# A linear-attention and mixture kernel: the last pair's product emitted unpinned behind its transfers, and the first batch's tail projections given the numerators' banks

## The chip, the cores and the metric

The kernel runs on one core of a Trainium2 chip. The metric is the time of one execution on the device in microseconds. The kernel before took a median of 893.23 us over 3 runs (892.91 to 893.44).

## What is computed

Three stages in a row, all from f32 inputs that reach the kernel as 64-bit words, with results as precise as f32 products of split operands:

```python
def phi(x):                                   # x: (4, 8, 576, 64)
    proj = np.einsum('bhsd,df->bhsf', x, w_phi)
    proj = proj - np.max(np.abs(proj), axis=-1, keepdims=True)
    return np.concatenate([np.exp(proj), np.exp(-proj)], axis=-1)
q_p, k_p = phi(q), phi(k)
kv  = np.einsum('bhsf,bhsd->bhfd', k_p, v)
num = np.einsum('bhsq,bhqd->bhsd', q_p, kv)
den = np.einsum('bhsf,bhf->bhs', q_p, np.sum(k_p, axis=2))[..., None] + 1e-06
x = (num / den)                               # tokens x (8 heads * 64) = 2304 x 512
h = np.maximum(np.maximum(x @ w1, x @ w2), x @ w3)   # 2304 x 768
x = h @ w_out                                        # 2304 x 512
h = x @ w_in                                         # 2304 x 2048
g = np.maximum(h, 0.0) + alpha * np.minimum(h, 0.0)
out = g @ w_out2                                     # 2304 x 512
```

## The kernel before

**Pairs.** The attention runs over 16 pairs: four batches of four pairs of heads, numbered in that order (`pairs`, loop at L467 to L489). Each pair has a keys part (`keys`, L267 on), which projects the keys (`exp_keys`, L226 on), takes their exponentials and sums up the product with the values in one PSUM bank, `kvp` (L293 for batch 0, whose matmuls take f32 as it is; L306 for the others, which take high and low halves), and a queries part (`queries`, L335 on), which projects the queries, transposes them (`pt`, L368), multiplies them into numerators `pn` (`num`, L346), and makes the denominators: rows of `nd` go by DMA into `dc` (L388), `V.tensor_scalar` adds an epsilon (L390), `V.reciprocal` inverts (L391), one DMA writes `dc` to `r_d` in HBM (L393), four DMAs read it back, broadcast over 64 partitions, into two tiles `xr` (L400). The product of `nd` and `xr` is x (`make_x`, L408 on: product L414, high half on ACT L421 through L64, low half on DVE L422 through L70). The 576 tokens of a head go as two groups of 256 and a tail of 64, and the tails of queries and keys share one projection, made in the keys part (L248 and L249).

**PSUM.** Eight banks: tag `pj` has 2 (projections, `project` L204 to L213), `p1` has 3, `pn`, `pt` and `kv` one each. In batch 0 `num` takes its bank from `p1`; later batches take it from `pn`, and `p1` serves the first expert layer (`layer1`, L436 on).

**Layer 1.** 48 units of 36 matmuls (L265, tile `p`), one unit for a batch, half of its 576 tokens (`c`) and 128 of the 768 features. A unit takes three banks: those of `p1`, or where `spread` is set those of `pn`, `pt` and `kv`. ACT copies the first bank (`s1`, L450), DVE takes the maximum with the second (L451) and with the third (`ho`, L453), POOL issues the write to `h_d` (L455). Units 0 to 33 are spread over the pair loop, units 34 to 47 follow it (L635 on). The units of batch 3 (36 on) need x of all four pairs of that batch, the last of which is pair 15's.

**Weight words.** Beside the units of the last loop, the weights of the later layers are read and converted. `stage` (L502) issues a DMA of 512 KB into one of three buffers `st`; `from_f64` (L74 to L87) turns it into f32 `wt` in four steps (ACT L77, DVE L84, ACT L80, DVE L86, from which the buffer is free again); then `split` makes high and low halves (`wo`, L64 on ACT and L70 on DVE), or `both` and `park` write combinations to `q_d` (L526, L539). The buffers lie where the keys' tiles lay (`ap_ctx.close()`, L490), so the second and third DMA wait for the last pair's last `kvp` matmul.

**Order.** A scheduler with a simulated timeline sets the order of each engine's instructions from priorities: `queries(last)` of the last pair is emitted at the priority NOW (L492, L493), conversions at LATER (L644). `tc.keep_in_program_order` takes one instruction out of that: it stays where the program has it.

```python
        waiting.append((pair, nd[0], raw))
        if pair[0] == 0 or pair[1] == NPAIR - 1 and pair != pairs[-1]:
            make_x(False)
...
    for u in range(3 * (len(pairs) - NPAIR) - LAG, 12 * B):
        c, f = u // NF1 % 2, u % NF1
        layer1(u // 12, c, f, xs[u // 12], w[f], u % 2 == 0)
        if waiting:
            make_x()
            lp_ctx.close()
```

So for batch 0 and for the last pair of a batch the product is emitted unpinned inside `queries`, and for the very last pair it is emitted pinned behind unit 34.

Of the kernel before, what the change touches and what calls it, by code (L numbers as in the profile page):

```python
# [23 lines left out]
NPAIR = H // 2  # L24
# [23 lines left out]
def tile_kernel(ctx: ExitStack, tc: tile.TileContext, qT, kT, tails, v, w_phi, w1, w2, w3, w_out, w_in, w_out2, alpha, out):  # L48
# [40 lines left out]
    def run(*steps):  # L89

        steps = list(steps)
        while steps:
            for x in list(steps):
                if next(x, x) is x:
                    steps.remove(x)
# [13 lines left out]
    def bank(tag, bufs, nm):  # L109
        return ps.tile([P, 512], F32, tag=tag, bufs=bufs, name=nm)  # L110
# [4 lines left out]
    ap_ctx, lp_ctx = ExitStack(), ExitStack()  # L115
# [76 lines left out]
    def features(pair, what):  # L192

        x = raws[pair, what]
        if plain(pair):
            return ((x, wraw),)
        tag, n, bufs = ("t", 2 * ST, 1) if what == "t" else ("", SM, 2)
        xh = at([P, n], F32R, tag="xh" + tag, bufs=bufs, name="xh" + what)
        xl = at([P, n], F32R, tag="xl" + tag, bufs=bufs, name="xl" + what)
        hi_dve(xh, x)  # L200
        sub(V, xl, x, xh)
        return ((xh, wph), (xh, wpl), (xl, wph))

    def project(ops, tiles):  # L204

        n = len(tiles)
        pj = bank("pj", 2, "pj")
        for i, t in enumerate(tiles):
            products(pj[:, i * 256 : (i + 1) * 256], [(x[:, t * P : (t + 1) * P], y) for x, y in ops])
        pv = pj[:, : n * 256].rearrange("p (a f) -> p a f", f=P)  # L210
        mx = at([P, 4], F32, tag="mx", bufs=4, name="mx")[:, : 2 * n]
        V.tensor_reduce(mx, pv, axis=AX.X, op=ALU.max, apply_absolute_value=True, negate=True)  # L212
        return pv, mx  # L213

    def less_max(pv, mx, dst):
        V.tensor_tensor(dst, pv, mx.unsqueeze(2).to_broadcast([P, mx.shape[1], P]), op=ALU.add)
# [8 lines left out]
    def exp_keys(pair):  # L225

        ops = features(pair, "k")
        for g, tiles in enumerate(GROUPS):
            pv, mx = project(ops, tiles)
            if i_of(pair) < len(CONVERT_IN) and g == 0:  # L230
                begun[pair] = at([P, 1], F32, tag="begun", bufs=2, name="begun")
                V.tensor_copy(begun[pair], mx[:, :1])
            e = at([P, 1024], F32, tag="e", bufs=2, name="ke")
            ev = e.rearrange("p (a s f) -> p a s f", s=2, f=P)
            if pair[0] == 0:
                pp = at([P, 4, P], F32, tag="pp", bufs=2, name="pp")
                less_max(pv, mx, pp)
                A.activation(ev[:, :, 0], pp, AF.Exp)
                A.activation(ev[:, :, 1], pp, AF.Exp, scale=-1.0)
                yield tiles, e  # L240
                continue
            my = at([P, 4], F32, tag="my", bufs=4, name="my")
            V.tensor_scalar(my, mx, -1.0, None, op0=ALU.mult)
            for a in range(4):
                A.activation(ev[:, a, 0], pv[:, a], AF.Exp, bias=mx[:, a : a + 1])  # L245
                A.activation(ev[:, a, 1], pv[:, a], AF.Exp, bias=my[:, a : a + 1], scale=-1.0)  # L246
            yield tiles, e
        pp = at([P, 2, P], F32, tag="ppt", bufs=1, name="ppt")  # L248
        less_max(*project(features(pair, "t"), (0,)), pp)  # L249
        tail_of[pair] = pp  # L250
        e = at([P, 1024], F32, tag="e", bufs=2, name="ke")[:, :512]
        ev = e.rearrange("p (a s f) -> p a s f", s=2, f=P)
        for i in range(2):
            A.activation(ev[:, :, i], pp, AF.Exp, scale=signs[:, i : i + 1])
        yield (4,), e
# [79 lines left out]
    def queries(pair):  # L335

        parts = ("q",) if plain_kv(pair) else ("qh", "ql")
        qf = []
        for n, (o, w) in enumerate(CHUNKS):
            qf.append([])  # L340
            for x in parts:
                tag = f"qh{n}" if x != "ql" and pair[1] % 2 * len(x) != 1 else f"ql{n}"
                qf[n].append(at([P, 2, 2, w], F32 if plain_kv(pair) else F32R, tag=tag, bufs=1, name=x))
        nd = [at([P, S], F32, tag="nd", bufs=3, name="nd") for _ in range(2)]

        def num(n):  # L346
            o, w = CHUNKS[n]
            kv = kvs_of[pair]
            for h in range(2):
                pn = bank("p1", 3, "pn") if pair[0] == 0 else bank("pn", 1, "pn")  # L350
                ops = []
                for s in range(2):
                    q_ = [t[:, h, s] for t in qf[n]]
                    k_ = [t[:, h, s] for t in kv]
                    ops += [(k_[0], x) for x in q_] + [(x, q_[0]) for x in k_[1:]]
                products(pn[:, :w], ops)
                A.activation(nd[h][:, o : o + w], pn[:, :w], AF.Copy)  # L357

        def tail():
            yield 2, (0,), tail_of[pair]  # L360

        for g, tiles, pp in chain(project_queries(pair), tail()):
            o, w = (0, 2 * P, SM)[g], ST if g == 2 else 2 * P
            pt = bank("pn" if pair[0] == 0 and g == 1 else "pt", 1, "pt")
            for i in range(len(tiles)):
                for h in range(2):
                    c = h * len(tiles) * P + i * P
                    nc.tensor.transpose(pt[:, c : c + P], pp[:, 2 * i + h], ident)  # L368
            n = min(g, 1)
            dst = [t[:, :, :, o - CHUNKS[n][0] : o - CHUNKS[n][0] + w] for t in qf[n]]  # L370
            if plain_kv(pair):
                e = dst[0]
            else:
                e = at([P, 2, 2, 256], F32, tag="qe", bufs=2, name="qe")[:, :, :, :w]
            pv = pt[:, : 256 * len(tiles)].rearrange("p (h s) -> p h s", h=2)[:, :, -w:]
            A.activation(e[:, :, 0], pv, AF.Exp)
            A.activation(e[:, :, 1], pv, AF.Exp, scale=-1.0)
            if not plain_kv(pair):
                (hi_dve if g == 1 else hi_act)(dst[0], e)
                sub(V, dst[1], e, dst[0])  # L380
            yield
            if g != 1:
                num(n)
        yield
        dc = at([P, S // D], F32, tag="dc", bufs=2, name="dc")
        for h in range(2):
            dr = D * (1 - h)
            nc.gpsimd.dma_start(dc[h * D : (h + 1) * D], nd[h][dr : dr + 1].rearrange("a (p n) -> a p n", p=D))  # L388
        nc.gpsimd.dma_start(nd[0][D:], nd[1][D:])
        V.tensor_scalar(dc, dc, EPS, None, op0=ALU.add)  # L390
        V.reciprocal(dc, dc)  # L391
        rows = r_d[pair[0], pair[1]]
        nc.gpsimd.dma_start(rows.rearrange("h (p n) -> (h p) n", p=D), dc)  # L393
        raw = []
        for c in range(2):
            xr = raw_tile()
            for h in range(2):
                r = slice(h * D, (h + 1) * D)
                src = rows[h : h + 1, c * CH : (c + 1) * CH]
                nc.gpsimd.dma_start(xr[r], src.to_broadcast([D, CH]))  # L400
            raw.append(xr)
        waiting.append((pair, nd[0], raw))
        if pair[0] == 0 or pair[1] == NPAIR - 1 and pair != pairs[-1]:
            make_x(False)

    waiting = []
# [50 lines left out]
    pairs = [(b, pr) for b in range(B) for pr in range(NPAIR)]  # L457
# [33 lines left out]
    sp = ctx.enter_context(tc.tile_pool(reuse_waits="tile", name="sp", bufs=1, side="right"))  # L491
    with tc.high_priority(offset=NOW):  # L492
        run(queries(last))  # L493

    def granule(pool, nm):

# [138 lines left out]
    for u in range(3 * (len(pairs) - NPAIR) - LAG, 12 * B):  # L635
        c, f = u // NF1 % 2, u % NF1
        layer1(u // 12, c, f, xs[u // 12], w[f], u % 2 == 0)
        if waiting:
            make_x()
            lp_ctx.close()  # L640
            ring2 = ctx.enter_context(tc.tile_pool(reuse_waits="tile", name="ring2", bufs=10, side="right"))
            hp_ctx = ExitStack()
            hp = hp_ctx.enter_context(tc.tile_pool(reuse_waits="tile", name="hp", bufs=1, side="right"))
        with tc.high_priority(offset=LATER):  # L644
            convert(2)
        if u == 12 * B - NF1 - 1:
            for kk in range(NF1 // 2):
                load_h(0, kk)
            for kk in range(NF1 // 2):
                early.append(fetch_h(1, kk))  # L650
# [210 lines left out]
    for block in range(nblocks):  # L861
# [31 lines left out]
        p1, u2, u3 = tmp("p1s"), tmp("u2"), tmp("u3")  # L893
# [66 lines left out]
```

## Time and profile before

| what | us |
|---|---|
| runs: median (lowest to highest, 3 runs) | 893.23 (892.91 to 893.44) |
| profiled execution | 893.7 |
| its span (granted TensorE clock 0.994) | 891.9 |
| PE busy | 867.6 (97%) |
| DVE busy | 652.7 (73%) |
| ACT busy | 510.4 (57%) |
| POOL busy | 144.2 (16%) |
| layer-1 matmuls (L265, `p<-x,w123t`), 1728 | 256.6 |
| idle time of PE just before them | 12.1, of which 10.8 behind the high half of x on ACT |

The profiled execution's own time is 1.8 us above its span. PE is TensorE, DVE VectorE, ACT ScalarE, POOL GpSimd, SP the queue that issues most DMAs. Busy is the time of the engine's instructions; "idle before" names what ended an engine's idle time.

### The profile page before, as it was taken

How to read it: one execution, taken by the hardware profiler on the slowest of the kernel's cores; microseconds unless marked ns; L12 is line 12 of the kernel's file. 1: busy time of each engine (PE TensorE's matmuls, PEld its weight loads, DVE VectorE, ACT ScalarE, POOL GpSimd, SP SyncE). 2: the span in 40 equal slices, each digit the busy share in tenths (PEclk: the TensorE clock that was granted, in tenths of full speed). 3: DMA queues.
4: the chain of work that ended last, by engine and by line, in shares of the span. 5: the costliest groups of instructions: out<-in, count | busy, mean ns of one | idle time of the engine just before them, and what ended most of it. 6: DMA issues, size and time to landing. Idle time of an engine off the chain costs nothing.

```text
span 891.9 us, 17549 instructions
## 1 busy us (share of the span) xinstructions
PE 867.6 (97%) x6667; PEld 856.5 (96%) x6667; DVE 652.7 (73%) x1238; ACT 510.4 (57%) x1037; POOL 144.2 (16%) x250
## 2 busy tenths in 40 slices
PE   9988999999999999959999999999999999999998
PEld 8878999999999999959999999999999999999998
DVE  6688889878777757769863464656468999988781
ACT  3665765776756656566853354646467663544440
POOL 0355222213122132311000111011111100000000
PEclk9999999999999999989999999999999999999999
DMA  6454553223222138997555573655347755543321
GB/s 206 127 189 148 181 171 95 85 70 89 84 83 69 34 112 305 347 320 241 154 184 187 187 232 112 211 189 187 120 158 259 259 185 174 158 143 119 119 71 48
DMA packets 72227, 142.98 MB, mean 160 GB/s; under 512 B 9152, under 2 KB 36176, under 8 KB 72144
## 3 DMA queue, kind: packets, MB, share of 16 engines
q1 hardware_dynamic: 57696, 100.29, 35.1%
q0 software_dynamic: 12576, 37.92, 12.5%
q10 hardware_dynamic: 1872, 3.67, 1.3%
q8 instruction: 52, 0.85, 0.4%
q14 instruction: 31, 0.25, 0.1%
HBM read 93.07 MB, written 46.34 MB: 156 GB/s over the span
## 4 chain that ended last, share of the span: by engine, by line
PE 86%; DVE 5%; DMA 5%; ACT 2%; issue 2%; DVEq 0%; ACTq 0%
PE acc L879 20%; PE p L265 20%; PE sums L791 11%; PE p L693 9%; PE pc L791 6%; PE pj L265 5%; PE pn L265 5%; DMA st<-in_w_out 3%; PE kvp L306 3%; PE pb L791 3%; PE kvp L293 3%; PE pt L368 2%; DVE mx L212 1%; DVE wt L86 1%; DMA st<-in_w_in 1%
## 5 line engine op out<-in xcount | busy, mean ns | idle before, releaser
L265 PE MATMUL p<-x,w123t 128*128 128x288 f32 x1728 | 256.6, 300 | 12.1 <-ACT x L64 10.8
L265 PEld LDWEIGHTS p<-x,w123t 128*128 128x128 f32 x1728 | 237.6, 190 | 13.8 <-ACT x L64 11.0
L791 PE MATMUL sums<-x,wi 128*128 128x288 f32 x768 | 107.6, 295 | 0.0
L879 PE MATMUL acc<-wq,o 128*128 128x256 f32 x864 | 105.5, 283 | 0.0
L879 PEld LDWEIGHTS acc<-wq,o 128*128 128x128 f32 x864 | 104.2, 189 | 0.0
L791 PEld LDWEIGHTS sums<-x,wi 128*128 128x128 f32 x768 | 103.9, 188 | 0.0
L879 PE MATMUL acc<-wq,x 128*128 128x256 f32 x648 | 78.1, 280 | 0.0
L879 PEld LDWEIGHTS acc<-wq,x 128*128 128x128 f32 x648 | 77.0, 188 | 0.0
L693 PE MATMUL p<-x,wo 128*128 128x288 f32 x576 | 76.6, 295 | 0.0
L693 PEld LDWEIGHTS p<-x,wo 128*128 128x128 f32 x576 | 76.5, 188 | 0.0
L810 DVE SCALAR_TENSOR_TENSOR g<-neg,al,g 128x576 f32<-128x576 f32 x64 | 50.3, 812 | 23.6 <-ACT neg L809 23.6
L212 DVE TENSOR_REDUCE mx<-pj 128x4 f32<-128x512 f32 (+1 forms) x80 | 50.2, 631 | 11.2 <-PE pj L265 9.2
L799 ACT ACTIVATE s<-sums 128x576 f32<-128x576 f32 x48 | 31.0, 646 | 42.0 <-PE sums L791 41.9
L455 POOL DMA_DIRECT2D h_d<-ho x48 | 28.1, 586 | 158.0 <-DVE ho L453 112.3
L357 ACT ACTIVATE nd<-pn 128x256 f32<-128x256 f32 (+1 forms) x64 | 26.9, 422 | 42.0 <-PE pn L265 26.7
L811 POOL DMA_DIRECT2D g_d<-g x32 | 22.9, 715 | 165.9 <-DVE g L810 149.1
L245 ACT ACTIVATE ke<-pj,mx 128x128 f32<-128x128 f32 x96 | 36.7, 383 | 15.1 <-DVE mx L212 15.1
L77 ACT ACTIVATE wt<-st 128x512 f16<-128x512 bf16 x38 | 30.1, 795 | 24.3 <-DMA st<-in_w_out 19.6
L809 ACT ACTIVATE neg<-g 128x576 f32<-128x576 f32 x64 | 40.2, 675 | 6.2 <-DVE g L841 5.9
L293 PE MATMUL kvp<-v,ke 128*128 128x128 f32 x320 | 42.3, 276 | 0.3 <-ACT ke L246 0.3
L64 ACT ACTIVATE o<-wt 128x512 fp32r<-128x512 f32 x45 | 27.4, 627 | 25.5 <-PE acc L879 15.1
L400 POOL DMA_DIRECT2D xr<-r_d x64 | 34.0, 537 | 46.2 <-DMA r_d<-dc 25.1
(160 smaller groups left out, 1808.1 us busy)
## 6 DMA issues: line engine op xcount, KB each, us to landing
g_d<-g POOLq DMA_DIRECT2D x32, 576.0 KB, 3.8
a<-g_d SPq DMA_DIRECT2D x36, 512.0 KB, 4.4
st<-in_w_out SPq DMA_DIRECT2D x22, 512.0 KB, 5.6
wst<-in_w SPq DMA_DIRECT2D x18, 512.0 KB, 4.7
st<-in_w_in SPq DMA_DIRECT2D x16, 512.0 KB, 4.2
yr<-y_d SPq DMA_DIRECT2D x28, 288.0 KB, 3.4
v<-in_v SPq DMA_DIRECT2D x16, 480.0 KB, 4.2
q_d<-wt SPq DMA_DIRECT2D x28, 256.0 KB, 7.0
```

Source lines behind the costliest of these rows:

```text
L77: order(A.activation(half[:, :, 1].bitcast(F16), lanes[:, :, 3].bitcast(BF16), AF.Copy))
L212: V.tensor_reduce(mx, pv, axis=AX.X, op=ALU.max, apply_absolute_value=True, negate=True)
L245: A.activation(ev[:, a, 0], pv[:, a], AF.Exp, bias=mx[:, a : a + 1])
L265: nc.tensor.matmul(dst, x, y, start=i == 0, stop=i == len(ops) - 1, **kw)
L293: nc.tensor.matmul(kvp[:, j * P : (j + 1) * P], e[:, c], rv[:, t, j // 2 : j // 2 + 2].rearrange("p a d -> p (a d)"), start=first, stop=t ...
L400: nc.gpsimd.dma_start(xr[r], src.to_broadcast([D, CH]))
L693: nc.tensor.matmul(p2[m // 2][1][:, m % 2], x, y, start=k + n == 0, stop=k == NF1 - 1 and n == 2)
L791: nc.tensor.matmul(dst[:, j], a, b, start=start and n == 0, stop=n == len(ops) - 1, skip_group_check=True)
L799: A.activation(s, src, AF.Copy)
L809: A.activation(neg, gv[:, j], AF.Relu, scale=-1.0)
L810: V.scalar_tensor_tensor(gv[:, j], neg, al[:, f + j : f + j + 1], gv[:, j], op0=ALU.mult, op1=ALU.add)
L879: nc.tensor.matmul(acc[i], x, y, start=half == 0 and f == 0 and n == 0 and place[i][1] == 0, stop=half == 1 and f == 3 and n == 2, skip_gr ...
```

## The change

Two edits. First, `project` has a new argument `spare`; where it is set the bank comes from tag `p1` (3) and not from `pj` (2), and the tails' projection sets it in batch 0, where `p1` otherwise holds the numerators. Second, the last pair's `make_x` is now emitted inside `queries(last)`, right behind the transfers into `xr`, unpinned and at the priority NOW, and the pools `ring2` and `hp`, which take the place of the queries' tiles, are opened behind it and not within the loop over units.

```diff
-    def project(ops, tiles):
+    def project(ops, tiles, spare=False):
 
         n = len(tiles)
-        pj = bank("pj", 2, "pj")
+        pj = bank("p1", 3, "pj") if spare else bank("pj", 2, "pj")
...
-        less_max(*project(features(pair, "t"), (0,)), pp)
+        less_max(*project(features(pair, "t"), (0,), pair[0] == 0), pp)
...
-        if pair[0] == 0 or pair[1] == NPAIR - 1 and pair != pairs[-1]:
+        if pair[0] == 0 or pair[1] == NPAIR - 1:
             make_x(False)
...
     with tc.high_priority(offset=NOW):
         run(queries(last))
+    lp_ctx.close()
+    ring2 = ctx.enter_context(tc.tile_pool(reuse_waits="tile", name="ring2", bufs=10, side="right"))
+    hp_ctx = ExitStack()
+    hp = hp_ctx.enter_context(tc.tile_pool(reuse_waits="tile", name="hp", bufs=1, side="right"))
...
         layer1(u // 12, c, f, xs[u // 12], w[f], u % 2 == 0)
-        if waiting:
-            make_x()
-            lp_ctx.close()
...
```

The scheduler then places many instructions anew. Three places follow. In the first, PE around the last pair's `kvp` (here `kvp_4632`); `p1_…` are the banks of units of layer 1, one bank for 12 matmuls, `pn_4661` is the last but one pair's numerators. Before, then after:

```order
1300 L265 MATMUL p1_4111<-x_2737,w123t_903 128x288 x3
1301 L265 MATMUL p1_4111<-x_3108,w123t_903 128x288 x3
1302 L265 MATMUL p1_4111<-x_3479,w123t_903 128x288 x3
1303 L306 MATMUL kvp_4632<-kh_4769,vh_2061 128x256
1304 L306 MATMUL kvp_4632<-kh_4769,vl_2062 128x256
1305 L265 MATMUL p1_4111<-x_3704,w123t_903 128x288
1306 L265 MATMUL pn_4661<-qh_4599,kvh_4452 128x256
...
1315 L306 MATMUL kvp_4632<-kh_4769,vl_2062 128x256
1316 L306 MATMUL kvp_4632<-kl_4770,vh_2061 128x256
1317 L265 MATMUL p1_4111<-x_3704,w123t_903 128x288
```

```order
1300 L265 MATMUL p1_4085<-x_3479,w123t_703 128x288 x3
1301 L265 MATMUL p1_4085<-x_3704,w123t_703 128x288 x2
1302 L306 MATMUL kvp_4632<-kh_4769,vh_2061 128x256
1303 L306 MATMUL kvp_4632<-kh_4769,vl_2062 128x256
1304 L265 MATMUL p1_4085<-x_3704,w123t_703 128x288
1305 L265 MATMUL p1_4098<-x_2737,w123t_895 128x288 x2
1306 L265 MATMUL pn_4661<-qh_4599,kvh_4452 128x256
...
1309 L306 MATMUL kvp_4632<-kh_4769,vl_2062 128x256
1310 L306 MATMUL kvp_4632<-kl_4770,vh_2061 128x256
1311 L265 MATMUL pn_4661<-ql_4600,kvh_4452 128x256
```

The last `kvp` matmul moves ahead, from inside bank `p1_4111` to inside the bank two before it: 935 matmuls of layer 1 stand ahead of it before, 914 after, and five of the six numerator matmuls `pn_4661` now stand behind it. The total of PE's instructions ahead of the first use of the last pair's x (behind 1350 matmuls of layer 1) is the same in both.

In the second, DVE around the last pair's denominators (`dc_5058`) and product (`xr_5065`, `xr_5068`); `wt_5767` is the 19th weight tile's conversion, `wt_5896` the 23rd; `s1_5263` and `ho_5266` are the evictions of the first unit that needs the last pair's x. Before, then after:

```order
641 L453 TENSOR_TENSOR ho_5119<-p1_5103,s1_5116 128x288
642 L390 TENSOR_SCALAR dc_5058<-dc_5058 128x9
...
656 L84 TENSOR_SCALAR wt_5896<-st_5782 128x512
657 L414 TENSOR_TENSOR xr_5065<-nd_4970,xr_5065 128x288
658 L86 TENSOR_TENSOR wt_5896<-wt_5896,st_5782 128x512
659 L70 TENSOR_TENSOR x_5123<-xr_5065,x_5123 128x288
...
672 L70 TENSOR_TENSOR wo_5841<-wt_5842,wo_5841 128x512
673 L451 TENSOR_TENSOR s1_5263<-p1_5237,s1_5263 128x288
674 L451 TENSOR_TENSOR s1_5326<-p1_5300,s1_5326 128x288
```

```order
645 L84 TENSOR_SCALAR wt_5767<-st_5614 128x512
646 L390 TENSOR_SCALAR dc_5058<-dc_5058 128x9
...
656 L84 TENSOR_SCALAR wt_5896<-st_5782 128x512
657 L414 TENSOR_TENSOR xr_5065<-nd_4970,xr_5065 128x288
658 L86 TENSOR_TENSOR wt_5896<-wt_5896,st_5782 128x512
...
664 L451 TENSOR_TENSOR s1_5263<-p1_5237,s1_5263 128x288
665 L70 TENSOR_TENSOR x_5076<-xr_5068,x_5076 128x288
666 L453 TENSOR_TENSOR ho_5266<-p1_5250,s1_5263 128x288
667 L70 TENSOR_TENSOR wo_5701<-wt_5702,wo_5701 128x512
```

The product stands at the same row behind the same conversion step. The denominators' addition stands four rows later, now behind a step of the 19th conversion, and the maximum on the first unit's bank stands ahead of the six low halves `wo` and not behind them. On ACT the copy `s1_5263` (L450) likewise moves from behind the six high halves `wo` to ahead of them.

In the third, DVE at the second weight conversion of the first batch (`wt_516`, which waits for the DMA into `wst_512`; `wst_335` belongs to the one before it); `mx_417` and `pp_409` read a projection of keys or queries. Before, then after:

```order
42 L84 TENSOR_SCALAR wt_516<-wst_512 128x512
43 L67 CAST xhq_535<-q_185 128x512
44 L70 TENSOR_TENSOR xlq_536<-q_185,xhq_535 128x512
45 L67 CAST xhk_558<-k_346 128x512
46 L212 TENSOR_REDUCE mx_417<-pj_410 128x4
47 L212 TENSOR_REDUCE mx_442<-pj_435 128x4
```

```order
42 L67 CAST xhq_535<-q_185 128x512
43 L212 TENSOR_REDUCE mx_417<-pj_410 128x4
44 L82 TENSOR_SCALAR wst_335<-wst_335 128x512
45 L70 TENSOR_TENSOR xlq_536<-q_185,xhq_535 128x512
46 L84 TENSOR_SCALAR wt_516<-wst_512 128x512
47 L216 TENSOR_TENSOR pp_409<-pj_410,mx_417 128x512
```

The conversion step moves behind four instructions that do not need it. On SP, some of the first batch's weight transfers (L181) and pair transfers (L150) change places; from the last pair's `kvp` on, SP's order is the same.

## Rows read from the trace of the kernel before

**Rows 1.** Busy time, share of the span and instructions of each engine, whole span.

```profile
PE 867.6 (97%) x6667; PEld 856.5 (96%) x6667; DVE 652.7 (73%) x1238; ACT 510.4 (57%) x1037; POOL 144.2 (16%) x250
```

**Rows 2.** Busy by window; last columns granted clock, DMA share, GB/s.

```profile
389.00:399.90 10.90, 0.12 (x1) 0.00 (x0) 5.17 (x10) 6.10 (x11) 2.08 (x4) 0.71 0.91 290
399.90:405.70 5.80, 4.43 (x18) 4.20 (x18) 5.73 (x13) 5.58 (x12) 0.00 (x0) 0.66 0.76 241
340.00:389.00 49.00, 49.00 (x370) 48.88 (x368) 37.15 (x81) 29.08 (x53) 13.08 (x23) 1.00 0.98 354
100.00:340.00 240.00, 240.00 (x1856) 237.56 (x1855) 186.59 (x389) 157.66 (x388) 56.53 (x102) 1.00 0.33 96
0.00:100.00 100.00, 91.58 (x635) 83.62 (x636) 77.64 (x182) 58.66 (x149) 34.17 (x61) 1.00 0.54 169
405.70:891.90 486.20, 482.46 (x3792) 482.26 (x3792) 340.37 (x568) 253.33 (x428) 38.33 (x60) 1.00 0.50 167
```

**Rows 3.** Chain of work that ended last: start, us, what.

```profile
326.77 0.47 PE kvp L306 x4
...
392.61 5.38 DMA st<-in_w_in
...
405.70 47.89 PE p L265 x360
```

**Rows 4.** Timeline of PE: start, busy, instruction, idle before and releaser.

```profile
399.92 4.43 PE L265 MATMUL p<-x,w123t 128*128 128x288 f32 x18 [10.80 <-ACT x L64]
405.70 9.55 PE L265 MATMUL p<-x,w123t 128*128 128x288 f32 x70 [1.35 <-ACT s L450]
```

**Rows 5.** Timeline of DVE, same columns.

```profile
384.99 0.16 DVE L390 TENSOR_SCALAR dc<-dc 128x9 f32<-128x9 f32 x1
...
385.42 0.21 DVE L391 RECIPROCAL dc<-dc 128x9 f32<-128x9 f32 x1
...
387.52 0.47 DVE L84 TENSOR_SCALAR wt<-st 128x512 uint16<-128x512 uint16 x1 [0.63 <-DMA st<-in_w_out]
...
398.09 0.46 DVE L84 TENSOR_SCALAR wt<-st 128x512 uint16<-128x512 uint16 x1 [1.38 <-DMA st<-in_w_in]
398.44 0.44 DVE L414 TENSOR_TENSOR xr<-nd,xr 128x288 f32<-128x288 f32 x1
```

**Rows 6.** Timeline of ACT.

```profile
399.44 0.76 ACT L64 ACTIVATE x<-xr 128x288 fp32r<-128x288 f32 x2
...
402.14 3.21 ACT L64 ACTIVATE wo<-wt 128x512 fp32r<-128x512 f32 x6
405.26 0.69 ACT L450 ACTIVATE s<-p 128x288 f32<-128x288 f32 x2
```

**Rows 7.** Timeline of POOL.

```profile
386.08 0.54 POOL L393 DMA_DIRECT2D r_d<-dc  x1
...
391.08 2.08 POOL L400 DMA_DIRECT2D xr<-r_d  x4 [3.92 <-DMA r_d<-dc]
```

**Rows 8.** DMA issues, 320 to 410 us: queue, count, KB, median us to landing.

```profile
xr<-r_d POOLq DMA_DIRECT2D x12, 72.0 KB, 5.1
```

**Rows 9.** Transfers into all tiles xr, same stretch.

```profile
DMA to landing us min/median/max: 2.2/4.5/7.3
```

**Rows 10.** Timeline of PE in the first batch, and one wait in the second.

```profile
34.33 0.36 PE L265 MATMUL pj<-wph,xht 128*128 128x256 f32 x1 [0.53 <-DVE pp L216]
...
48.95 0.35 PE L265 MATMUL pj<-wph,xht 128*128 128x256 f32 x1 [1.52 <-DVE pp L216]
...
50.75 0.36 PE L265 MATMUL pj<-wph,xhq 128*128 128x256 f32 x1 [0.77 <-DVE pp L216]
...
60.43 0.38 PE L265 MATMUL pj<-wph,xhk 128*128 128x256 f32 x1 [1.62 <-ACT ke L246]
...
81.35 0.35 PE L265 MATMUL pj<-wph,xht 128*128 128x256 f32 x1 [2.09 <-DVE pp L216]
```

**Rows 11.** Timeline of DVE in the first batch.

```profile
29.47 0.48 DVE L84 TENSOR_SCALAR wt<-wst 128x512 uint16<-128x512 uint16 x1 [3.93 <-DMA wst<-in_w]
```

More of the change, by code (lines that the diff above doesn't have):

```diff
@@ L637, in tile_kernel @@
         layer1(u // 12, c, f, xs[u // 12], w[f], u % 2 == 0)
-        if waiting:
-            make_x()
-            lp_ctx.close()
-            ring2 = ctx.enter_context(tc.tile_pool(reuse_waits="tile", name="ring2", bufs=10, side="right"))
-            hp_ctx = ExitStack()
-            hp = hp_ctx.enter_context(tc.tile_pool(reuse_waits="tile", name="hp", bufs=1, side="right"))
         with tc.high_priority(offset=LATER):
```

## Prediction

> **What bounds the kernel now.** I first read the busy line of the page: PE has 867.6 us of work [rows 1], so only PE's idle time, some 24 us, can be won, unless its work becomes cheaper or dearer. The view by windows then says where that idle time lies [rows 2]. Between 100 and 340 us PE works without a gap, and so it does from 340 to 389 us; from 405.7 us to the end it lacks 486.2 - 482.5 = 3.7 us. Two holes remain: the first 100 us, where it lacks 8.4 us, and 389 to 405.7 us, where it does 4.55 us of work in 16.7.
>
> The chain of waits goes through the second hole [rows 3]: the last pair's last `kvp` matmul at 326.77 us, then weight transfers into `st` and their conversions, up to the one that lands at 397.99 us, and layer 1 again at 405.70 us. The timeline of PE shows the hole as two waits [rows 4]: 10.80 us until 399.92 us for the high half of x, then 18 matmuls, then 1.35 us until 405.70 us for the copy `s1`. The reader should see on DVE why the first is so long [rows 5]: the last pair's product (L414, 398.44 us) stands right behind the first conversion step of the 23rd weight tile (L84, 398.09 us), which waits for that tile's DMA. And on ACT why there is a second [rows 6]: the copies `s1`, which free the first unit's bank, start at 405.26 us, behind six high halves `wo` of 3.21 us together. In 340 to 389 us the DMA engines are busy 98% of the time [rows 2]: the conversions go at the pace of the transfers, whose landing ended DVE's wait at the 19th tile and at the 23rd alike [rows 5].
>
> The 18 matmuls cost 4.43 us, 246 ns each, where those of 340 to 389 us cost 49.00/370 = 132 ns [rows 2]: the granted clock is 0.71 and then 0.66 in the hole, where PE goes from the 2.4 GHz level to that of 1.2 GHz after standing idle; from 405.70 us on a matmul takes 9.55/70 = 136 ns again [rows 4].
>
> **The change, late part.** Unpinning the product does not move it: it stands at the same row of DVE, behind the same conversion. What moves is the work ahead. The last `kvp` matmul stands 21 matmuls of layer 1 and five of the numerators earlier, and what PE does up to the hole is the same; so the ring of weight buffers, whose second and third transfer wait for that matmul, starts about 26 x 0.132 = 3.4 us earlier against the hole. SP's order from there on is unchanged. If the transfers are paced by their own bandwidth, the 23rd tile lands at 398.0 - 3.4 = 394.6 us.
>
> The product also needs its `xr`. The denominators' addition (L390, before at 384.99 us) now stands behind L84 of the 19th tile, before at 387.52 us [rows 5]; 3.4 us earlier that is 384.1, so addition and reciprocal, 0.64 us from start to end, are over by about 385.1 and POOL issues `r_d` (before 386.08 us) then. Its return took 5.0 us until the first `xr` issue at 391.08 us [rows 7], so 390.1 now; the second half of the first tile goes out 0.5 later and lands after 5.1 us, the median [rows 8]: 395.7. So the product starts at 395.7 and not at 398.44: its own 0.45 and the high half with its latency, 0.48, let PE restart at 396.6 (before 399.92). The landing is the unknown here, between 2.2 and 7.3 us [rows 9]; I take the median of this very transfer. At 2.2 us the product goes by the ring instead (L84 done at 394.95), at 7.3 us it starts at 397.9.
>
> The Trainium skill, page "DMA: Bandwidth & Descriptors", in the section on SWDGE's anatomy, fits a software-queue DMA by 2.0 us plus its bytes over 436 GB/s, an estimate of 2.2 us for the 72 KB here. By it the sum of the late part would be -5.4; the median row speaks against it, with transfers beside it that load the engines above 0.9.
>
> From 396.6 the 18 matmuls take 4.43 us as before and end at 401.1. Now the copy and the maxima on the first unit's bank stand ahead of the `wo` halves on ACT and DVE. The first unit's share of them is nine, done 2.2 us into the 18; the copy, 0.35 us, ends near 399.4, the two maxima near 399.9 and 400.8 (they stand behind L86 of the 24th tile, which is 3.4 earlier too). Each is before 401.1, so PE goes on at once, where before it did so at 405.70: **-4.6 us**. Bounds: -5.4 by the ring alone, -2.4 with slow landings; if the ring gains nothing and only the second wait goes, PE restarts at 399.9 + 4.43 = 404.35, which is -1.35, call it -1.2 with a late eviction. If the clock held, half of the 4.43 would go as well, 2.0 more; nothing in the rows suggests it, since PE would still stand idle some 7 us.
>
> The six `wo` halves, some 3.2 us of ACT and of DVE, come later by a few tenths than the evictions, and are needed only by the next layer. The pools opened earlier move no transfer.
>
> **The change, early part.** In the first batch the tails' projections waited for one of the two `pj` banks twice, 0.53 and 1.52 us, released by L216 on DVE [rows 10]. With a bank of `p1` both waits go: **-2.0 us**. The numerators share the three banks, and use one at a time for 12 matmuls or fewer, so I cost their side at nothing; if they wait once for a bank that a tail holds, the nearest row is the longest wait of this kind, 2.09 us (a tail of batch 1, which is not changed), so the loss is bounded by +0.1 net. On the other side, DVE's conversion step L84, which stalled it 3.93 us for a DMA [rows 11], now stands behind work that needs no DMA. PE has no gap at that moment, so nothing is won there directly, but DVE's lag is what the later waits are made of: all five waits of [rows 10] together are 6.5 us, the most that can be won. On SP some weight and pair transfers of the first batch change places; I cost that at nothing, since none of the PE waits of [rows 10] is ended by a DMA, and what it may lose is within the same bound of 2.09 us a wait. PE works without a gap from 100 us on, so what is won early moves everything behind it.
>
> **Sum:** -4.6 - 2.0 = -6.6. The profiled execution took 893.7 us, so 887.1; the median of the runs lies 0.5 lower, so I forecast **886.6 us**. 0.2% is 1.8 us, about what a measurement of this kernel can tell from no change.
>
> **The rivals.**
> *Only the evictions count* (20%): the ring goes at the pace of all transfers, so an earlier start is used up by others that share the DMA engines (98% busy), and the 23rd tile lands no earlier. Then -1.2 - 2.0 = -3.2, 890.0 us. For it: the share; against it: the same bytes lie between start and hole, and PE does the same work beside them.
> *The early part is other than two waits* (17%): the banks change DVE's order and nothing is won (-4.6, 888.6 us), or all five waits go (-4.6 - 6.5 = -11.1, 882.1 us), which I hold for much the rarer.
> *Slower, by the denominators* (8%): L390 now hangs on the 19th tile. If the ring starts no earlier, that step is at 387.5 and the reciprocal is over at 388.5; with both hops at the slow end of 7.3 us and 0.5 for the second issue the product starts at 388.5 + 7.3 + 0.5 + 7.3 = 403.6, plus waits at issue 404.1. PE restarts at 405.0 and goes on at 409.5: +3.8 in the late part, and the time is 895.0 us with the early waits gone, 897.0 with nothing won there. It loses as soon as the product starts later than 398.44 + 1.9 = 400.3, since the second wait, 1.35, and the shorter way to the high half, 0.55, are won in any case. Medians of 5.0 and 5.1 would give 399.1, so both hops must be slower than seen at the median.
> *Nothing is moved* (10%): the change means to free the product, yet it stands behind the 23rd conversion as before; if the ring is not earlier and the numerators' banks give back what the tails win, the time is 893 us, within 1.8.
>
> **How the numbers follow.** The forecast's case, both parts roughly as worked out, 885 to 888.5 us, gets 45%; the rivals as above. Faster by more than 1.8 us are the forecast, the first two rivals: 82%; same 10%; slower 8%. From 883 to 892 us the range holds the forecast's bounds, the first rival and most of the second; outside lie the slow one, most of the unmoved one and the best early case.
>
> **What would show it right or wrong.** Right: the last `kvp` matmul some 3.4 us of PE's work further ahead of the hole; L390 right behind L84 of the 19th tile; the product no later than 396 us less the early gain; one wait of about 7.5 us in place of 10.80, and none for `s1` behind 18 matmuls; `wo` behind `s1_5263`; no wait of a tail `xht` for L216 in the first 60 us, and PE's lack in the first 100 us down from 8.4 to about 6.4. Wrong: the 23rd tile landing at the same distance from the last `kvp`'s old place, a product that waits for DMA `xr` past 398 us, a wait of `pn` for a bank in the first 60 us, or any new gap between 100 and 389 us, where evictions stand beside the conversions.

## The result, and the profile after

The changed kernel takes 887.76 us (median; 886.39 to 888.98, 6 runs) beside 893.73 us before on the same chip: a ratio of 0.9919, 95% interval 0.9891 to 0.9947, so by the ratio 7.2 us faster, between 4.7 and 9.7; the medians lie 6.0 us apart. The forecast was 886.6 us against 893.23, so -6.6 us, faster by more than 0.2%. It held.

The profiled execution has a span of 885.4 us, 6.5 less than before. The busy line of the page answers to [rows 1]; the work is the same, only the time beside it has shrunk:

```profile
PE 868.8 (98%) x6667; PEld 857.9 (97%) x6667; DVE 651.8 (74%) x1238; ACT 510.0 (58%) x1037; POOL 145.4 (16%) x250
```

The view by windows, cut at the places that answer to [rows 2] (columns: window, length, then busy time and count of PE, PEld, DVE, ACT, POOL, then granted clock, DMA share, GB/s):

```profile
0.00:100.00 100.00, 94.31 (x653) 86.27 (x653) 79.50 (x191) 60.29 (x154) 36.37 (x62) 1.00 0.59 176
100.00:336.00 236.00, 236.00 (x1827) 233.58 (x1826) 184.52 (x382) 156.38 (x384) 55.31 (x101) 1.00 0.33 98
336.00:386.00 50.00, 50.00 (x377) 50.00 (x377) 38.38 (x82) 30.13 (x56) 13.14 (x24) 1.00 1.00 348
386.90:394.10 7.20, 0.03 (x2) 0.02 (x1) 2.80 (x6) 3.27 (x6) 1.18 (x3) 0.71 1.00 304
394.10:400.10 6.00, 6.00 (x25) 6.00 (x26) 5.24 (x12) 5.03 (x10) 0.56 (x1) 0.50 0.83 248
400.10:885.40 485.30, 481.52 (x3787) 481.31 (x3785) 340.80 (x569) 254.22 (x430) 37.98 (x59) 1.00 0.51 167
```

PE lacks 5.7 us in the first 100 (8.4 before), nothing up to 386.9 us, 7.2 us in one hole, and 3.8 us to the end, as before. The second wait of the hole is gone. What remains of the hole's price stands in the clock column: 0.50 for the 6 us after it.

The chain, then PE, DVE, ACT and POOL at the hole (each of a view of its own; start, duration, what, and in brackets the idle time before and what ended it), answering to [rows 3 to 7]:

```profile
321.12 0.48 PE kvp L306 x4
...
386.04 6.11 DMA st<-in_w_in
...
394.08 52.97 PE p L265 x378
```

```profile
394.08 18.19 PE L265 MATMUL p<-x,w123t 128*128 128x288 f32 x115 [7.17 <-ACT x L64]
```

```profile
381.82 0.17 DVE L390 TENSOR_SCALAR dc<-dc 128x9 f32<-128x9 f32 x1
...
392.24 0.46 DVE L84 TENSOR_SCALAR wt<-st 128x512 uint16<-128x512 uint16 x1 [2.11 <-DMA st<-in_w_in]
392.59 0.44 DVE L414 TENSOR_TENSOR xr<-nd,xr 128x288 f32<-128x288 f32 x1
...
397.09 0.45 DVE L451 TENSOR_TENSOR s<-p,s 128x288 f32<-128x288 f32 x1
```

```profile
393.04 0.65 ACT L80 ACTIVATE st<-st 128x512 uint32<-128x512 uint16 x1
393.60 0.76 ACT L64 ACTIVATE x<-xr 128x288 fp32r<-128x288 f32 x2
...
396.40 0.41 ACT L450 ACTIVATE s<-p 128x288 f32<-128x288 f32 x1 [0.32 <-PE p L265]
...
397.56 3.22 ACT L64 ACTIVATE wo<-wt 128x512 fp32r<-128x512 f32 x6
```

```profile
382.53 0.55 POOL L393 DMA_DIRECT2D r_d<-dc  x1 [5.90 <-DVE dc L391]
...
385.92 2.16 POOL L400 DMA_DIRECT2D xr<-r_d  x4 [1.04 <-DMA r_d<-dc]
```

The single wait is 7.17 us in place of 10.80 and 1.35, and the 18 matmuls run on into the next ones (115 in a row up to the end of the stretch shown). The product (392.59 us) still starts directly behind L84 of the 23rd tile (392.24 us). On ACT the copy `s1` (396.40 us) now stands ahead of the six `wo` (397.56 us); before it stood behind them. The transfers into `xr`, issued from 385.92 us on, land as follows, beside [rows 8, 9]:

```profile
DMA to landing us min/median/max: 4.9/5.4/6.8
```

The first two of these four fill the tile that the first product needs. By themselves:

```profile
DMA to landing us min/median/max: 4.9/5.0/5.0
```

The second of them is issued at 386.5 us, so the tile is complete at 391.5 us, 1.1 us before the product starts. Before the change it was complete at 395.3 us, 3.1 us before the product.

**Where the time went.** PE ran dry at 399.92 - 10.80 = 389.12 us before and at 394.08 - 7.17 = 386.91 now: 2.2 us won early in this execution. From there the same 18 + 70 matmuls were done at 405.70 + 9.55 = 415.25 us before, 26.1 us later; now the row of 115 ends at 412.27, less 27 x 0.136 = 3.7 for those beyond the 88, 408.6 us, 21.7 later: 4.4 us won at the hole. Together 6.6, the difference of the spans within 0.1.

The early part by the waits of PE in the first 130 us (waiting group, releaser, total, times, longest), against [rows 10]:

```profile
PE kvp L293 <- ACT ke L254: 1.2, 1, 1.2
...
PE pt L368 <- ACT q L377: 1.0, 1, 1.0
PE pj L265 <- DVE pp L216: 0.7, 1, 0.7
```

The tails' two waits for L216 in the first batch are gone, and others are there: the last `kvp` of a pair now waits 1.2 us for the tail's exponentials (L254 on ACT), a transposition 1.0 us for L377.

### The profile page after: what moved, and what is told of

Read it like the earlier page. It is cut to its first block, busy times and chain, and to the rows that moved or that the text cites. A ratio compares the mean times of both kernels' runs of the same rounds, so it can differ in the third digit from the quotient of the medians.

```text
span 885.4 us, 17562 instructions
## 1 busy us (share of the span) xinstructions
PE 868.8 (98%) x6667; PEld 857.9 (97%) x6667; DVE 651.8 (74%) x1238; ACT 510.0 (58%) x1037; POOL 145.4 (16%) x250
## 4 chain that ended last, share of the span: by engine, by line
PE 90%; DMA 5%; DVE 2%; ACT 1%; POOL 1%; issue 1%; SPq 0%; ACTq 0%; DVEq 0%
PE p L265 25%; PE acc L877 20%; PE sums L789 12%; PE p L691 9%; PE pc L789 6%; PE pn L265 5%; PE pj L265 4%; PE kvp L306 3%; PE pb L789 3%; PE kvp L293 2%; DMA dc<-nd 2%; PE pt L368 2%; DMA st<-in_w_out 1%; DMA xr<-r_d 1%; DMA st<-in_w_in 1%
## 5 line engine op out<-in xcount | busy, mean ns | idle before, releaser
L293 PEld LDWEIGHTS kvp<-v,ke 128*128 128x128 f32 x320 | 39.7, 191 | 2.5 <-ACT ke L254 1.4
```

Of the source, the lines that this page charges most:

```text
L293: nc.tensor.matmul(kvp[:, j * P : (j + 1) * P], e[:, c], rv[:, t, j // 2 : j // 2 + 2].rearrange("p a d -> p (a d)"), start=first, stop=t ...
```

## The experiments

**One edit at a time.** The first run takes the banks alone, the second the unpinned product and the moved pools alone (the pools' lines are those of the change and are left out below):

```diff
-        less_max(*project(features(pair, "t"), (0,)), pp)
+        less_max(*project(features(pair, "t"), (0,), pair[0] == 0), pp)
```

> The first edit alone: batch 0's tail projections take banks of p1; the last pair's product is emitted as before (pinned, behind unit 34). The instruction order of all five engines comes out the same as with both edits. Theory (the whole change is the first edit: its banks move the early work, and the new order moves the last kvp matmul and the evictions): -6.5 us against the kernel before, as with both edits, wait of PE for the last pair's x about 7.2 us, no second wait. Rival (the late part belongs to the second edit, the unpinned product): only the early part, -2 us, and a wait of about 11 us.

```diff
-        if pair[0] == 0 or pair[1] == NPAIR - 1 and pair != pairs[-1]:
+        if pair[0] == 0 or pair[1] == NPAIR - 1:
             make_x(False)
```

> The second edit alone: the last pair's product unpinned inside its queries, the pools opened behind it; the tails keep the two banks pj. The order of all engines comes out as in the kernel before. Theory: 0 us, within 0.2%, PE waits 10.8 us and then 1.35 us as before. Rival (the second edit carries the late part): -4.5 us.

The banks alone: 888.61 us, ratio 0.9932 (0.9910 to 0.9954). The product alone: 894.67 us, ratio 1.0010 (0.9985 to 1.0034). PE at the hole with the banks alone, then with the product alone:

```profile
398.20 12.07 PE L265 MATMUL p<-x,w123t 128*128 128x288 f32 x71 [6.98 <-ACT x L64]
```

```profile
399.26 4.69 PE L265 MATMUL p<-x,w123t 128*128 128x288 f32 x18 [9.31 <-ACT x L64]
405.04 5.19 PE L265 MATMUL p<-x,w123t 128*128 128x288 f32 x25 [1.09 <-ACT s L450]
```

The first has one wait of 6.98 us and no second; the second has both, as before. So the whole gain, the late part too, comes from the banks of the first batch. The second edit changes no instruction's place on any engine: in the traces the order with the banks alone is that of both edits, and the order with the product alone that of the kernel before. The first edit changes the order 300 us further on too; that it does so through the scheduler's simulated time is likely, but not shown. The theory holds, the rival falls.

**An early ring with the old order of evictions.** Only pair 3's tail takes a `p1` bank:

```diff
-        less_max(*project(features(pair, "t"), (0,), pair[0] == 0), pp)
+        less_max(*project(features(pair, "t"), (0,), pair == (0, 3)), pp)
```

> Both edits, but only pair 3's tail takes a p1 bank. The last kvp matmul now stands even earlier (909 matmuls of layer 1 ahead of it, against 914 and 935), but the evictions of the first unit stay behind the six wo halves as in the kernel before, and the product stands behind the first step of the 24th weight tile. Theory (ring start sets the product, evictions set the second wait): ring 4.2 us earlier than before against PE's work, 24th tile 2.5 us behind the 23rd, so PE goes on at x about 1.7 us earlier, and a second wait of about 1 us comes back: late part about -2.4 us, early part 0 to -2, so -2 to -4.5 us in all. Rival (an earlier ring is used up by contention, only the order of the evictions counts): late part 0 or +2 (24th tile).

891.89 us, ratio 0.9978 (0.9952 to 1.0003); the profiled execution has a span of 887.8 us. PE at the hole:

```profile
396.02 4.69 PE L265 MATMUL p<-x,w123t 128*128 128x288 f32 x18 [6.50 <-ACT x L64]
401.47 8.73 PE L265 MATMUL p<-x,w123t 128*128 128x288 f32 x64 [0.76 <-ACT s L450]
```

In this execution, the fastest of its ten, PE runs dry at 389.5 us, about where it did before, so nothing was won early; the first wait is 6.50 us with an earlier ring, and the second is back with 0.76. That fits the division of work that the prediction made: ring start for the first wait, order of the evictions for the second. In this trace the first wait is shorter than expected (6.5, not 9.1), because the transfers came sooner than the start alone explains: L84 of the 23rd tile 2.6 us after PE ran dry, where 4.2 off the 9.0 of before would be 4.8. The times, whose interval just reaches 1, show less of the gain than this one execution does; its size stays open, and the division between the two waits rests on this one trace.

**Holding the conversions behind the product.** In the changed kernel the product's data are complete at 391.5 us, but DVE, which goes in order, stands before the 23rd tile and starts the product at 392.59. Here the 17th tile's conversion waits for the product, by one column of its target written from `xr`:

```diff
         wt = word()
+        if len(sources) == 38 - 3 - 16:
+            V.tensor_copy(wt[:, :1], held[0][:, :1])
         run(from_f64(staged.pop(0), wt))
```

(`held` is the last pair's list of `xr`, kept by `make_x`.)

> The changed kernel, with the conversion of the 17th weight tile held until the last pair's product is made (one column of its wt is written from xr first), so that the product and the denominators stand behind no later tile. Theory (the product waits for its place behind the 23rd tile and not for its data): it starts when xr lands, about 389 us against 392.6; PE waits 3.5 to 4 us in place of 7.2: -3.5 us against the changed kernel, 1 to 2 more if the clock falls for a shorter time. Rival A (its data are as late as the tile): -1 us. Rival B (the held conversions come back as waits for evictions or weights between 400 and 450 us, where DVE is already busy 97%): 0 or slower.

882.32 us, ratio 0.9860 (0.9822 to 0.9898); measured twice more, 880.58 us, 0.9843 (0.9818 to 0.9868), and 879.96 us, 0.9851 (0.9828 to 0.9873). It beats both kernels. PE and DVE at the hole, and the landing of the transfers into `xr`:

```profile
390.01 2.98 PE L265 MATMUL p<-x,w123t 128*128 128x288 f32 x18 [0.32 <-ACT x L64]
393.66 16.53 PE L265 MATMUL p<-x,w123t 128*128 128x288 f32 x123 [0.67 <-ACT s L451]
```

```profile
382.76 0.17 DVE L390 TENSOR_SCALAR dc<-dc 128x9 f32<-128x9 f32 x1
...
389.02 0.46 DVE L415 TENSOR_TENSOR xr<-nd,xr 128x288 f32<-128x288 f32 x1 [5.52 <-DMA xr<-r_d]
389.51 0.15 DVE L523 COPY wt<-xr 128x1 f32<-128x1 f32 x1
```

```profile
DMA to landing us min/median/max: 2.2/2.5/2.6
```

The product now waits for its own data (5.52 us for DMA `xr`, which costs nothing: DVE has nothing else to free there) and PE for 0.32 and 0.67 us. The 18 matmuls take 2.98 us, where they took 4.43 before the change. The ratios (0.9919 for the changed kernel, 0.9843 to 0.9860 here) put the gain against the changed kernel at 5 to 7 us, where 3.5 was expected and up to 5.5 with the clock. The windows show two reasons; first this kernel, then the changed one:

```profile
386.00:388.00 2.00, 2.00 (x17) 2.00 (x17) 0.00 (x0) 0.00 (x0) 2.00 (x4) 1.00 0.18 58
388.00:390.00 2.00, 1.69 (x13) 1.45 (x11) 0.95 (x4) 0.49 (x2) 0.02 (x1) 1.00 0.35 90
390.00:392.00 2.00, 1.94 (x12) 1.70 (x13) 1.80 (x6) 2.00 (x4) 0.00 (x0) 1.00 0.00 0
```

```profile
386.00:388.00 2.00, 0.90 (x7) 0.67 (x6) 1.13 (x4) 0.70 (x2) 2.00 (x4) 1.00 0.94 343
388.00:390.00 2.00, 0.00 (x0) 0.00 (x0) 0.97 (x2) 1.38 (x2) 0.08 (x1) 0.98 0.97 237
390.00:392.00 2.00, 0.00 (x0) 0.00 (x0) 0.14 (x1) 0.00 (x0) 0.00 (x0) 0.50 0.98 320
```

The granted clock stays at 1.00, where it falls to 0.50 in the changed kernel. And with the weight ring stopped the DMA engines are busy 0.18 and 0.35 of the time, not 0.94 and 0.97, so `xr` lands in 2.5 us and not in 5.4. Counted from the moment PE runs dry, the product starts 6.4 us earlier than in the changed kernel (0.7 us before that moment and not 5.7 behind it). Of this 1.8 us come from `r_d`, which goes out 6.2 us ahead of that moment and not 4.4, 1.0 from its return (2.4 us and not 3.4), 2.5 from the landing of the first tile (2.5 us and not 5.0); the place behind the 23rd tile is the rest, 1.1. So the theory of this run names the smaller part: rival A was near the truth on the changed kernel, whose data were hardly ahead of the tile, and falls on the time, because the hold makes the data early as well. Of rival B there is a trace, a wait of 0.9 us at L694 for an eviction, far from giving the gain back. The rule of the Trainium skill that the prediction weighed (page "DMA: Bandwidth & Descriptors", anatomy of an SWDGE transfer), an estimate of 2.2 us for 72 KB, agrees with the 2.5 us of this run, where the engines are nearly free, and not with the 5.4 us beside a full ring.

**The hold without the banks.** The same hold, the tails on `pj`:

> The hold at the 17th tile without the first edit: the tails keep the two banks pj, so PE's order up to the last pairs is that of the kernel before, and the product is again made before the 17th conversion. It prices the early part by itself, against the run of the hold with both edits (882.3 us in the last call). Theory as predicted (the tails' banks are worth 2.0 us early): 884.5 us, and PE's waits of 0.4 to 0.5 and 1.3 to 1.5 us for L216 at the tails back in the profile. Rival (the first 50 us profiled so far show a new wait of numerators for the exponentials of queries, 1.25 and 1.84 us, in place of the tails' waits, so the banks are worth 0 to 1): 882.5 to 883.5 us. The ring starts 3.4 us later against PE's work, which should not matter once the product does not wait for it; if it does, 886 us or more.

> The hold at the 17th tile with both edits once more, beside the same kernel without the first edit: 882.3 us as in the last call, ratio to the kernel before 0.986; PE waits under 1.5 us between 380 and 400 us; the granted clock stays at 1.00 there.

887.99 us, ratio 0.9929 (0.9904 to 0.9955), 7.4 us behind the same hold with the banks (880.58). Neither 2 nor 1: the last clause of the expectation is what happened. PE here, and POOL here and in the hold with the banks:

```profile
394.00 4.02 PE L265 MATMUL p<-x,w123t 128*128 128x288 f32 x18 [4.62 <-ACT x L64]
```

```profile
384.51 0.55 POOL L393 DMA_DIRECT2D r_d<-dc  x1
...
389.91 2.09 POOL L400 DMA_DIRECT2D xr<-r_d  x4 [4.32 <-DMA r_d<-dc]
```

```profile
382.62 0.55 POOL L393 DMA_DIRECT2D r_d<-dc  x1 [4.32 <-DVE dc L391]
...
385.54 2.12 POOL L400 DMA_DIRECT2D xr<-r_d  x4 [1.84 <-DMA r_d<-dc]
```

PE runs dry at 389.38 us, 0.55 later than with the banks, so the early part is not the cause in these two profiles. The wait for x is 4.62 us against 0.81. From the issue of `r_d` to that of `xr` it takes 5.4 us here and 2.9 there, 2.5 of the 3.8 us by which the waits differ; the other 1.3 lie ahead of `r_d`, which goes out 4.9 us before PE runs dry here and 6.2 there. The ring starts 3.4 us later against PE's work, and the DMA engines are busy 0.73 of the stretch from `r_d` to `xr` here, 0.51 there, so its last transfers before the stop are likely still under way when `r_d` is written. I had thought that the start of the ring no longer mattered once the product did not stand behind it. It seems to, by way of the two hops; the old order of the other instructions, which comes with the late ring, was not tried apart from it.

**A later hold.** At the 20th tile, so that the denominators' addition stays behind the 19th:

> The changed kernel with the hold at the 20th tile in place of the 17th: the denominators' addition stays behind a step of the 19th conversion, as in the changed kernel (about 381.8 us), and only the product is freed from the 23rd. Theory (the place behind the 23rd tile costs the changed kernel what its data would not): xr is issued at about 386 us as there, lands in 3 to 5 us beside fewer weight transfers, product at 390 us against 392.6, so 2.5 us less wait, 885 us. Rival (what helped with the hold at the 17th tile was the earlier denominators alone): as the changed kernel, 887.5 us.

886.87 us, ratio 0.9911 (0.9886 to 0.9935), beside the changed kernel's 0.9919. PE at the hole:

```profile
392.61 4.36 PE L265 MATMUL p<-x,w123t 128*128 128x288 f32 x18 [2.73 <-ACT x L64]
398.72 13.53 PE L265 MATMUL p<-x,w123t 128*128 128x288 f32 x100 [1.75 <-ACT s L451]
```

The wait for x falls from 7.17 to 2.73 us, as expected and beyond, but the 18 matmuls run at the lower clock again (4.36 us), and a second wait of 1.75 us for `s1` appears. Ahead of the hole PE waits once for an eviction in this execution:

```profile
343.19 3.42 PE L265 MATMUL p<-x,w123t 128*128 128x288 f32 x23 [1.73 <-DVE ho L454]
```

From the moment PE runs dry (389.88 us) to the end it takes 495.1 us, 3.4 less than in the changed kernel's profile, but that moment comes 3.0 us later. By the times the kernel can't be told from the changed one, and its median lies between theory and rival: what the later hold is worth stays open.

**The denominators on GpSimd.**

```diff
-        V.tensor_scalar(dc, dc, EPS, None, op0=ALU.add)
-        V.reciprocal(dc, dc)
+        if pair == pairs[-1]:
+            G.tensor_scalar(dc, dc, EPS, None, op0=ALU.add)
+            m1 = at([P, S // D], F32, tag="one", bufs=1, name="one")
+            G.memset(m1, -1.0)
+            G.tensor_tensor(dc, dc, m1, op=ALU.pow)
+        else:
+            V.tensor_scalar(dc, dc, EPS, None, op0=ALU.add)
+            V.reciprocal(dc, dc)
```

> The hold at the 17th tile and, besides, the last pair's epsilon and inverse on GpSimd (an addition, and a power of minus one with a tile of minus ones) in place of DVE, so that they follow their own transfers and not DVE's evictions. Theory: r_d is issued at about 379 us and not at 383.5, xr lands before PE runs dry at 389.7, so the wait of 0.3 us for x goes, the 0.7 us for s1 may stay: -0.3 to -1 us against the hold alone, too little to tell by the times; the timeline tells it. Rival (GpSimd's queue is late at this place, its power slow): r_d no earlier, 0 or slower.

881.38 us, ratio 0.9843 (0.9816 to 0.9871), beside 0.9843 for the hold alone. POOL:

```profile
378.57 0.26 POOL L391 TENSOR_SCALAR dc<-dc 128x9 f32<-128x9 f32 x1
378.92 1.83 POOL L394 TENSOR_TENSOR dc<-dc,one 128x9 f32<-128x9 f32 x1
381.05 0.63 POOL L399 DMA_DIRECT2D r_d<-dc  x1 [0.30 <-POOL dc L394]
```

`r_d` goes out at 381.05 us, earlier than 382.62, and the wait for x is gone (one of 0.68 us for `s1` stays), as expected; not earlier still, because the power on 128 x 9 elements takes 1.83 us. The times can't tell it from the hold alone.

**The early part, with an early ring in both.** The hold with only pair 3's tail in a `p1` bank, beside the hold with all four:

> The hold at the 17th tile, with only pair 3's tail in a p1 bank. The last kvp matmul is early (909 matmuls of layer 1 ahead of it; 914 with all four tails, 935 with none), so the ring is early too, while the tails of pairs 0 to 2 keep the banks pj. It asks for the early part alone, without the late ring that spoiled that question in the run with none. Theory (the early part is worth little: the tails' waits go, but a wait of kvp for the tail's exponentials of 1.1 to 2.8 us comes instead, in all six profiles with four p1 tails): within 1 us of the hold with all four tails. Rival (the early part is worth the 2.0 us of the prediction, less the third tail's share): 1.3 to 2 us slower than that.

> The hold at the 17th tile with all four tails in p1 banks, for comparison on the same chip: 0.984 to 0.986 of the kernel before, a wait of kvp for the tail's exponentials of 1.1 to 2.8 us near 53 us, waits of 0.3 to 0.9 us for x and 0.7 us for s1 near 390 us.

881.98 us, ratio 0.9885 (0.9867 to 0.9903), against 879.96 us, 0.9851 (0.9828 to 0.9873). The waits at the hole are alike (0.22 and 0.65 us; 0.33 and 0.68), so the 2.0 us between the medians, 3.0 by the ratios, lie before it: PE runs dry at 392.6 and at 387.6 us in the two profiles. PE there, with three tails on `pj` and then with none:

```profile
392.78 2.97 PE L265 MATMUL p<-x,w123t 128*128 128x288 f32 x18 [0.22 <-ACT x L64]
```

```profile
387.92 2.95 PE L265 MATMUL p<-x,w123t 128*128 128x288 f32 x18 [0.33 <-ACT x L64]
```

The first of these is the slowest of its five executions (884.42 us), so the 5.0 us between the two moments overstate the difference. My theory falls and the rival, which was the prediction's own -2.0, stands: the two intervals overlap at their ends, but all five executions with one tail (881.79 to 884.42 us) are slower than all five with four (877.60 to 881.57).

## Why the prediction was right

**The ring's start: right, in size too.** From the end of the last pair's `kvp` matmuls to the moment PE runs dry it took 389.12 - 327.24 = 61.9 us before and takes 386.91 - 321.60 = 65.3 now: 3.4 us, the forecast's 26 x 0.132. L84 of the 23rd tile came 9.0 us after PE ran dry and comes 5.3 us after it now, 3.6 sooner. The rival in which the ring gains nothing is excluded by that.

**What the product waits for: wrong step, small price.** The prediction took `xr` as the later of the two, at 395.7 us on the scale of before. It was the ring: 392.59 + 2.2 = 394.8. The step that failed is the return of `r_d`, taken as 5.0 us and measured as 385.92 - 382.53 = 3.4; the landing, taken as 5.1, was 4.9 and 5.0 for the first tile. (That 5.1 was the median of the last three pairs together; the last pair's own four took 3.7 to 4.7 before, so the value fits better than its source.) But the high half of x was taken at 0.48 us behind the product, and ACT stood before it with L80 of the same tile, as it had before (393.04 to 393.60 us), so that PE went on 1.49 us after the product's start, not 0.93. The two deviations cancel, which is luck: PE restarted at 394.08 + 2.2 = 396.3 against 396.6.

**The evictions: right.** The copy `s1` at 396.40 us stands ahead of the `wo` and no second wait follows; where the old order of evictions is put back beside an early ring, 0.76 us of it returns.

**The clock: undersized.** The prediction priced only the 18 matmuls at the lower level. In the rows the clock is 0.50 until 400.1 us: 25 matmuls in 6 us, so seven beyond the 18 at some 240 ns and not 136, 0.7 us; the 18 themselves took 0.1 less than forecast. Against that stand the 0.3 us of the earlier restart; the late part came to some -4.4 and not to -4.6.

**The early part: about right in size, wrong as a sum of waits.** Both waits for `pj` went. In all seven profiles with four `p1` tails a wait of `kvp` for the tail's exponentials took their place, 1.1 to 2.8 us, and in six of them one of 0.2 to 1.8 us of the numerators for L376. So the -2.0 is not what two waits cost; what remains after the exchange comes to about as much by the times: 2 to 3 us for three of the four tails, and for the banks alone 6.1 by the ratio, or 4.9 by the medians, less the 4.4 at the hole, 1.7 or 0.5. One profile does not show it: PE ran dry between 386.9 and 391.2 us in six executions of this early order, and between 389.1 and 390.0 in three of the old one. So the rival in which nothing is won early is excluded by the pair of runs with one tail and four, and not by the change's own times.

**What the prediction did not separate** is which edit does the work. It said that unpinning does not move the product, and that the work ahead moves, but not by which edit. The runs of one edit each show that it is the banks, and that the unpinned product does nothing here.

**What stays open:** why the scheduler's new order puts the last `kvp` 26 matmuls earlier; only that it follows from the banks was shown. That numerators and tails share three banks without harm was not tried apart from the order it brings. How much of the late part is the ring's and how much the evictions', the times did not settle.

## What to carry to other kernels

Where a scheduler sets the order, compare the order that each edit gives alone before crediting either: here a change of banks in the first 60 us moved a transfer ring 300 us later, and the edit at that place moved nothing. An instruction whose data are ready pays for what stands ahead of it on an engine that goes in order, but look first when the data come: here they were 1.1 us ahead of the product. A data dependency that holds the stream of conversions behind the critical chain took PE's wait from 7.2 to 0.3 us, and most of that because the chain's own data came earlier: with the prefetch stopped, its small transfers landed in half the time.

## What was not expected of the hardware

The clock's fall isn't tied to the long hole alone. With the banks alone a wait of 1.81 us near 53 us is followed by a stretch at the lower level; in the profiled execution of the changed kernel, with the same order and a wait of 1.18 us, it is not. Windows of two microseconds, the banks alone and then the changed kernel:

```profile
52.00:54.00 2.00, 0.19 (x3) 0.01 (x1) 2.00 (x6) 0.57 (x2) 0.56 (x1) 1.00 0.02 3
...
56.00:58.00 2.00, 2.00 (x8) 1.71 (x8) 0.94 (x2) 2.00 (x9) 0.34 (x1) 0.50 0.96 262
```

```profile
52.00:54.00 2.00, 1.29 (x10) 1.19 (x11) 1.93 (x8) 1.85 (x6) 1.58 (x3) 1.00 0.18 51
...
56.00:58.00 2.00, 2.00 (x13) 1.60 (x12) 1.77 (x4) 2.00 (x6) 0.00 (x0) 1.00 0.98 270
```

PE's 2 us then hold 8 matmuls and not 13. Behind the waits of 1.6, 2.2 and 2.8 us of three other executions of this early order the clock fell too, behind 1.1 and 1.5 us in two it did not. The mean clock goes with the time in the kernel before (0.987 at 898.44 and 899.37 us, 0.996 at 891.27, of 25 executions), but it is not the whole spread: with the hold and the denominators on GpSimd, two executions at 1.000 took 878.59 and 882.01 us. After the hole it stayed at the lower level for 4.1 us of work before the change and for 6 us after it.
